# Two row blocks of an MLP's first layer by seven block products for eight, in a kernel that adds an FNet layer and an MLP

## The chip, the cores and the metric

The kernel runs on one core of a Trainium2 chip. The metric is the time of one execution in device microseconds (us). Engines are named as in the profile: PE is TensorE, DVE VectorE, ACT ScalarE, POOL GpSimd, SP the engine that issues most DMAs; ACT issues some.

## The reference

x has 2048 rows of 640. After a layer norm without scale or shift, two branches are added to x: the real part of a two-dimensional Fourier transform, given as matrices, and an MLP with 1536 hidden units.

```
xn = layernorm(x)
a, b = xn @ wr.T, xn @ wi.T                      # 640 x 640
y = cr @ a - ci @ b                              # 2048 x 2048
mlp = gelu(xn @ w1 + b1) @ w2 + b2               # tanh form of gelu
out = x + y + mlp
```

All is float32. A float32 product is made of three matmuls in the fp32r type: each operand is split into an upper half (a copy, rounded) and a lower half (the rest), and upper x upper, upper x lower and lower x upper are summed in PSUM (`product`, L269 to L274).

## The kernel before

The rows are worked on in four blocks of 512 (NT = 4, TB = 512), the hidden units in 12 groups of 128 (NF = 12), the 640 columns in 5 chunks of 128 (ND = 5). First the MLP runs for the four blocks, then the Fourier branch.

**MLP.** The main loop (L746 on) counts g from 0 to 47: block t and unit i. `hidden(g)` (L280) makes the first layer of one unit for one block in bank g % 3: 5 chunks x 3 matmuls of 128x512, one line, L292. `gelu(g)` (L301) has ACT apply gelu from PSUM into a buffer "ab", copy it to the upper half of "hs", and DVE subtract for the lower half. `output(g)` (L313) adds this unit's part of the second layer into banks 3 to 7: 5 x 3 matmuls. hidden runs two units ahead of output, so a unit goes hidden(g + 2), gelu(g + 2), output(g). Each engine executes its instructions in the order in which the program writes them; there is no scheduler.

The split weights W1 and W2 of all 12 units stay in SBUF from block 0 to the end of the MLP, in places (`PLACES`, L130) that the Fourier stages take over afterwards.

**Beside the MLP.** `background(t, i)` (L682) prepares the next block: rows of x are loaded (`load_x`), `ln_stats` takes their mean and variance on DVE, `ln_scale` one square root on ACT (which loads another table, and gelu's again), `ln_apply` normalises on DVE and stores each chunk of 128 rows to DRAM in four pieces, so 16 stores "xs" for a block, on SP. `load_z` reads them back in another order, and `transpose_z` and `prep_xt` turn and split them for the next block. For blocks 2 and 3 three of the four x chunks are loaded a block ahead, and 27 us or so lie between ln_apply and the first turn.

`prep_w(s)` (L381) has 15 steps in blocks 1 and 2 (`w_steps`, L743). They make seven forms of sums of the hidden transform's weights for each chunk j, for a seven-product scheme in the Fourier branch: step 3j turns two raw tiles on DVE and makes forms 0 and 1, step 3j + 1 forms 6 and 2, step 3j + 2 forms 3, 4 and 5. `put_w` (L366) makes one form: ACT copies the upper half into one of two buffers "wst", DVE subtracts, and ACT issues the store to DRAM ("wit"). Stores are issued in pairs at the end of a step's pair (`put_away`).

During block 3 `build` and `fourier_step` (L721) make the operands of the Fourier stages from the stored xs ("xab", "xc"), and store some to DRAM (forms_ab, forms_c).

At the end of a block `add_block` (L330) adds the bias on ACT in the bank, has DVE turn it into one of two buffers and POOL add it to the rows of x ("xo"), which go to DRAM ("ys").

Of the kernel before, what the change touches and what calls it, by code (L numbers as in the profile page):

```python
# [13 lines left out]
ALU = mybir.AluOpType  # L14
# [12 lines left out]
def kernel(  # L27
# [78 lines left out]
    def bank(k):  # L106
        return banks[:, k]
# [32 lines left out]
    ]  # L140
    slots = {}

    def place(tag, shape, dtype=F32R):

        return wpool.tile(list(shape), dtype, tag=tag, bufs=1, name=tag)
# [74 lines left out]

    def new_xt(t, j):
        XT[j] = mr.tile([P, 2, TB], F32R, tag="xt", bufs=ND, name=f"xt{t}_{j}")
# [8 lines left out]
    def transpose_z(t, j):  # L231
        zt[j] = mr.tile([P, TB], F32, tag="zt", bufs=2, name=f"zt{t}_{j}")
        nc.vector.transpose(
            zt[j].rearrange("p (n i) -> p n i", i=B), Z["z"][:, :, j * B : (j + 1) * B]
        )
# [41 lines left out]
    NG = NT * NF  # L277
    HT, oacc, xo = {}, {}, {}

    def hidden(g):  # L280
        i = g % NF
        acc = bank(g % 3)
        kinds = ((0, 0), (0, 1), (1, 0))
        steps = [(j, k) for j in range(ND) for k in range(3)]
        if g == 0:
            steps = FIRST
        if g == 1:

            steps.sort(key=lambda s: s[1] == 2)
        for n, (j, k) in enumerate(steps):  # L290
            a, b = kinds[k]
            nc.tensor.matmul(  # L292
                acc, W1[i][:, a, j * P : (j + 1) * P], XT[j][:, b], start=n == 0, stop=n == len(steps) - 1
            )
        return acc
# [5 lines left out]
    def gelu(g, acc, fill=lambda k: None):  # L301

        i = g % NF
        a = mr.tile([P, TB], F32, tag="ab", bufs=2, name=f"ab{g}")
        nc.scalar.activation(a, acc, AF.Gelu_apprx_tanh, bias=b1c[:, i : i + 1])  # L305
        fill(0)
        hs = mr.tile([P, 2, TB], F32R, tag="hs", bufs=3, name=f"hs{g}")
        HT[g] = hs
        nc.scalar.activation(hs[:, 0], a, AF.Copy)  # L309
        fill(1)  # L310
        nc.vector.tensor_tensor(hs[:, 1], a, hs[:, 0].bitcast(F32), op=ALU.subtract)  # L311

    def output(g):  # L313
        t, i = divmod(g, NF)
        if i == 0:
            oacc[t] = [bank(3 + e) for e in range(ND)]
        hs = HT[g]
        for e in range(ND):
            cols = slice(e * P, (e + 1) * P)
            product(  # L320
                oacc[t][e], (W2[i][:, 0, cols], W2[i][:, 1, cols]), (hs[:, 0], hs[:, 1]), i == 0, i == NF - 1
            )
# [7 lines left out]
    def add_block(dst, e, acc, name, eng=nc.gpsimd, bias=None, home=rows):  # L330

        if bias is not None:
            nc.scalar.activation(acc, acc, AF.Identity, bias=bias)
        yt = home.tile([P, TB], F32, tag="yt", bufs=2, name=name)
        nc.vector.transpose(yt, acc)
        d = dst[:, :, e * B : (e + 1) * B]
        eng.tensor_tensor(d, d, yt.rearrange("p (n i) -> p n i", i=B), op=ALU.add)
# [4 lines left out]
    def load_w(m, j):  # L342

        t = A["w"].tile([P, EB, B], F32, tag=f"wraw{m}", bufs=1, name=f"wraw{m}_{j}")
        A["wraw", m] = t
        v = (wr, wi)[m].rearrange("(n r) d -> r n d", r=B)
        for q in range(Q):
            s0 = q * DQ + j * B
            nc.sync.dma_start(t[q * B : (q + 1) * B], v[:, :, s0 : s0 + B])

    def turn_w(m, j):
        t = A["w"].tile([P, D], F32, tag=f"wt{m}", bufs=1, name=f"wt{m}_{j}")
        A["wt", m] = t
        nc.vector.transpose(
            t.rearrange("p (c q i) -> p q c i", q=Q, i=B),
            A.pop(("wraw", m)).rearrange("p (q c) i -> p q c i", q=Q),
        )

    stores = []
# [6 lines left out]
    def put_w(w, j, main, odd=None, negative=False):  # L366

        n = GWIDE[w] * P
        t = A["w"].tile([P, 2, 3 * P], F32R, tag="wst", bufs=2, name=f"wst{w}_{j}")
# [11 lines left out]
    def prep_w(s):  # L381
# [4 lines left out]
        if k == 0:  # L386
            turn_w(0, j)
            turn_w(1, j)
            if j + 1 < ND:
                load_w(0, j + 1)  # L390
                load_w(1, j + 1)
# [137 lines left out]
    def load_xr(k):  # L529
# [4 lines left out]
        if k in (0, len(builds) - 1):  # L534
            n = 2 if k else 0
            A["xcp", n] = place(f"xc{n}{n + 1}", (P, 2, 2, 7 * P))
# [9 lines left out]
    def build(k, what="abc"):  # L546
        h, c = builds[k]
        b0, b1_ = [r.rearrange("p (q c i) -> p c q i", q=Q, i=B) for r in xr[k]]
        if k == 0:
            A["sums"] = out_pool.tile([P, 2, 9 * P], F32, tag="zo", bufs=1, name="sums")  # L550
        if k < NK:
            A["xab", c] = place(f"xab{c}", (P, 2, 10 * P))
        A["xc", c] = A["xcp", c // 2 * 2 if h == 0 else 0][:, c % 2]
        ab, xc = A["xab", c], A["xc", c]
        tmp = A["sums"][:, k % 2]
# [40 lines left out]

    zeros = rows.tile([P, TB], F32, tag="yt", bufs=2, name="zeros")
# [25 lines left out]
    for tag, size, keys in PLACES:  # L623
        t = place(tag, (P, size // 4))
# [15 lines left out]
    scratch = mr.tile([P, 2 * TB], F32, tag="hs", bufs=3, name="scratch")[:, :D]  # L640
# [41 lines left out]
    def background(t, i):  # L682

        if t == 1 and i == 0:
            es_e.close()
            A["es"] = ExitStack()
            A["w"] = pool("wrawp", stack=A["es"])
            load_w(0, 0)
            load_w(1, 0)
        if t + 1 < NT:  # L690
            c0 = (t + 1) * NC

            s = 2 if t == 0 else 0
            if t == 0 and i < 2:
                ln_apply(2 * i)
                ln_apply(2 * i + 1)
                load_x(c0 + 2 * i)
                load_x(c0 + 2 * i + 1)
            elif t > 0 and i == 0:
                load_x(c0 + 3)  # L700
            if s <= i < s + 4:
                ln_stats(c0 + i - s)
            if i == s + 4:
                ln_scale(c0, 4)
                for c in range(c0, c0 + 4):
                    ln_apply(c)
                load_z(t + 1)
                if t + 2 < NT:
                    for c in range(c0 + 4, c0 + 7):
                        load_x(c)  # L710
            if i in (8, 9):
                transpose_z(t + 1, i - 8)
        if t == 3 and i == 0:
            A["es"].close()
            A["raw"] = pool("rawp")
            load_xr(0)
            load_xr(1)
            load_a(0)
            load_a(1)

    def fourier_step(i):  # L721
        if 2 <= i < 2 + 2 * NK:
            k = i - 2
            build(k, "abc" if i < 9 else "a")
            if k < NK:
                nc.sync.dma_start(forms_ab[k], A["xab", k].bitcast(F32))
                nc.sync.dma_start(forms_c[k], A["xc", k].bitcast(F32))
            load_xr(k + 2)
        if i == 9:
            A["r01"] = place("r01", (P, 2, 2, 2, TB), F32)  # L730
            turn(0, 0)
            turn(0, 1)
            A["as"] = place("as", (P, 3, 2, 2, TB))
        if i == 10:
            form(0)
            turn(1, 0)
            turn(1, 1)
            form(1)
        if i == 11:
            form(2)  # L740


    w_steps = [(1, i) for i in (1, 2, 3, 3, 5, 6, 7)] + [(2, i) for i in (0, 1, 2, 3, 5, 5, 6, 7)]  # L743
    gelu(0, acc0)
    gelu(1, acc1)
    for g in range(NG):  # L746
# [6 lines left out]
        background(t, i)  # L753
        if i == 10 and t + 1 < NT:
            load_xo(t)
        if i == NF - 1:
            acc = hidden(g + 2) if g + 2 < NG else None
            output(g)
            if acc is None:

                fourier_step(i)
                break

            def fill(k):
                for e in ((0,), (1, 2))[k]:
                    add_block(xo[t], e, oacc[t][e], f"ot{t}_{e}", bias=b2c[:, e : e + 1])

            gelu(g + 2, acc, fill)
            for e in (3, 4):
                add_block(xo[t], e, oacc[t][e], f"ot{t}_{e}", bias=b2c[:, e : e + 1])  # L770
            for k, (c0, c1) in enumerate(YCOLS):
                nc.sync.dma_start(ys[k][t], xo[t][:, :, c0:c1])
        elif i == NF - 2:
            output(g)
            if g + 2 < NG:
                gelu(g + 2, hidden(g + 2))
        else:
            acc = hidden(g + 2)
            if i == NF - 3 and t + 1 < NT:
                for j in range(ND):  # L780
                    prep_xt(t + 1, j)
                    if j + 2 < ND:
                        transpose_z(t + 1, j + 2)
            gelu(g + 2, acc)
            output(g)
        if t == 3 and i < NF - 1:
            fourier_step(i)
        for k, step in enumerate(w_steps):
            if step == (t, i):
                prep_w(k)  # L790
# [60 lines left out]
    for e in range(ND):  # L851
# [461 lines left out]
```

## Time and profile before

| | us |
|---|---|
| runs shown: median, lowest, highest | 860.79, 860.23, 860.89 |
| span of the profiled execution | 858.6 |
| median less that span: starting and ending | 2.2 |
| 15 matmuls (one unit, one layer) | 3.40 |
| blocks 1 to 3, from unit 0 to unit 0 | 81.6 |

The profile lists each engine's busy time, the chain of work that ended last, and groups of instructions with their mean duration (ns) and the idle time of their engine ahead of them, with what ended it. A matmul is shown with 389 ns, but they overlap in the array; one starts every 227 ns. In rows of the timeline the columns are start, length (us), engine, line, operation, output<-input, form, count, and in brackets the idle time ahead and what ended it. ACTq and SPq are the queues in which DMAs are issued. The profiled execution's own time is not listed beside its span; the three runs' median stands for it.

### The profile page before, as it was taken

How to read it: one execution, taken by the hardware profiler on the slowest of the kernel's cores; microseconds unless marked ns; L12 is line 12 of the kernel's file. 1: busy time of each engine (PE TensorE's matmuls, PEld its weight loads, DVE VectorE, ACT ScalarE, POOL GpSimd, SP SyncE). 2: the span in 40 equal slices, each digit the busy share in tenths (PEclk: the TensorE clock that was granted, in tenths of full speed). 3: DMA queues.
4: the chain of work that ended last, by engine and by line, in shares of the span. 5: the costliest groups of instructions: out<-in, count | busy, mean ns of one | idle time of the engine just before them, and what ended most of it. 6: DMA issues, size and time to landing. Idle time of an engine off the chain costs nothing.

```text
span 858.6 us, 10232 instructions
## 1 busy us (share of the span) xinstructions
PE 850.2 (99%) x3747; PEld 703.1 (82%) x3747; DVE 624.1 (73%) x792; ACT 335.7 (39%) x468; POOL 21.0 (2%) x22
## 2 busy tenths in 40 slices
PE   8999999999999999999999999999999999999997
PEld 6888888888888888888888888888888888888885
DVE  7554555366443678989989787998977998885687
ACT  7354434255333555443434344232322423223241
POOL 0000300030003000000000000000000000000000
PEclk9999999999999999999999999999999999999999
DMA  6656476875457984949753659954765879804364
GB/s 184 198 164 175 97 176 189 215 153 174 141 165 169 319 358 86 218 105 216 167 151 86 184 159 266 237 127 107 176 186 172 260 177 230 313 19 177 123 170 105
DMA packets 208625, 152.34 MB, mean 177 GB/s; under 512 B 82368, under 2 KB 182976, under 8 KB 208064
## 3 DMA queue, kind: packets, MB, share of 16 engines
q1 hardware_dynamic: 196336, 138.98, 62.4%
q10 hardware_dynamic: 12240, 12.72, 4.2%
q8 instruction: 29, 0.48, 0.2%
q14 instruction: 20, 0.16, 0.1%
HBM read 108.67 MB, written 42.99 MB: 177 GB/s over the span
## 4 chain that ended last, share of the span: by engine, by line
PE 98%; DMA 0%; DVE 0%; SPq 0%; issue 0%; ACT 0%; DVEq 0%; ACTq 0%
PE banks L273 26%; PE banks L272 26%; PE banks L274 26%; PE banks L292 19%; DMA x<-in_A_x_dram 0%; PE banks L635 0%; DVE st L185 0%; SPq L178 0%; DVE yo L1278 0%; DVE mv L186 0%; DVE xp L208 0%; ACT mv L192 0%; DVE mv L194 0%; DVE mv L195 0%; DVE mv L197 0%
## 5 line engine op out<-in xcount | busy, mean ns | idle before, releaser
L274 PE MATMUL banks<-as,xab 128*128 128x512 f32 x407 | 158.4, 389 | 0.0
L272 PE MATMUL banks<-as,xab 128*128 128x512 f32 x407 | 158.3, 389 | 0.0
L273 PE MATMUL banks<-as,xab 128*128 128x512 f32 x407 | 158.3, 389 | 0.0
L160 ACT ACTIVATE as<-r 128x1024 fp32r<-128x1024 f32 x80 | 85.0, 1062 | 173.1 <-PE banks L274 148.6
L161 DVE TENSOR_TENSOR as<-r,as 128x1024 fp32r<-128x1024 f32 x80 | 97.2, 1216 | 38.9 <-ACT as L160 38.9
L292 PE MATMUL banks<-xt,xab 128*128 128x512 f32 x420 | 99.1, 389 | 0.0
L311 DVE TENSOR_TENSOR hs<-ab,hs 128x512 fp32r<-128x512 f32 x48 | 36.5, 760 | 78.5 <-ACT hs L309 78.5
L292 PEld LDWEIGHTS banks<-xt,xab 128*128 128x128 f32 x420 | 78.7, 188 | 16.5 <-DVE xt L161 0.2
L272 PEld LDWEIGHTS banks<-as,xab 128*128 128x128 f32 x407 | 76.4, 188 | 16.0
L273 PEld LDWEIGHTS banks<-as,xab 128*128 128x128 f32 x407 | 76.4, 188 | 15.9
L274 PEld LDWEIGHTS banks<-as,xab 128*128 128x128 f32 x407 | 76.4, 188 | 15.8
L272 PE MATMUL banks<-as,xc 128*128 128x512 f32 x224 | 87.1, 389 | 0.0
L273 PE MATMUL banks<-as,xc 128*128 128x512 f32 x224 | 87.1, 389 | 0.0
L274 PE MATMUL banks<-as,xc 128*128 128x512 f32 x224 | 87.1, 389 | 0.0
L305 ACT ACTIVATE ab<-banks,b1c 128x512 f32<-128x512 f32 x48 | 33.0, 689 | 96.3 <-PE banks L292 91.8
L160 ACT ACTIVATE as<-rt 128x1024 fp32r<-128x1024 f32 x32 | 34.0, 1063 | 70.6 <-PE banks L274 57.9
L292 PE MATMUL banks<-xt,as 128*128 128x512 f32 x240 | 57.0, 389 | 0.0
L292 PEld LDWEIGHTS banks<-xt,as 128*128 128x128 f32 x240 | 45.0, 188 | 9.4
L272 PEld LDWEIGHTS banks<-as,xc 128*128 128x128 f32 x224 | 42.0, 188 | 8.8
L273 PEld LDWEIGHTS banks<-as,xc 128*128 128x128 f32 x224 | 42.0, 188 | 8.7
L274 PEld LDWEIGHTS banks<-as,xc 128*128 128x128 f32 x224 | 42.0, 188 | 8.7
L272 PE MATMUL banks<-hs,xc 128*128 128x512 f32 x120 | 46.7, 389 | 0.0
(170 smaller groups left out, 1365.5 us busy)
## 6 DMA issues: line engine op xcount, KB each, us to landing
raw<-in_A_dft_seq_re_dram SPq DMA_DIRECT2D x64, 256.0 KB, 5.9
raw<-in_A_dft_seq_im_dram SPq DMA_DIRECT2D x64, 256.0 KB, 5.4
wit<-wst ACTq DMA_DIRECT2D x20, 384.0 KB, 3.5
ws<-wit SPq DMA_DIRECT2D x15, 384.0 KB, 4.4
x<-in_A_x_dram SPq DMA_DIRECT2D x16, 320.0 KB, 4.3
xs<-x SPq DMA_DIRECT2D x64, 80.0 KB, 1.8
xo<-in_A_x_dram SPq DMA_DIRECT2D x16, 320.0 KB, 6.1
forms_ab<-xab SPq DMA_DIRECT2D x4, 1280.0 KB, 5.9
```

Source lines behind the costliest of these rows:

```text
L160: nc.scalar.activation(h, s, AF.Copy)
L161: nc.vector.tensor_tensor(l, s, h.bitcast(F32), op=ALU.subtract)
L272: nc.tensor.matmul(acc, wh, mh, start=first, stop=False, skip_group_check=goes_on)
L273: nc.tensor.matmul(acc, wh, ml, start=False, stop=False, skip_group_check=goes_on)
L274: nc.tensor.matmul(acc, wl, mh, start=False, stop=last, skip_group_check=goes_on)
L292: nc.tensor.matmul(acc, W1[i][:, a, j * P : (j + 1) * P], XT[j][:, b], start=n == 0, stop=n == len(steps) - 1)
L305: nc.scalar.activation(a, acc, AF.Gelu_apprx_tanh, bias=b1c[:, i : i + 1])
L311: nc.vector.tensor_tensor(hs[:, 1], a, hs[:, 0].bitcast(F32), op=ALU.subtract)
```

## The change

Blocks 0 and 1 stay as they are, but units 0 and 1 come last in block 1. For blocks 2 and 3 the first layer is made for both at once. Of the 5 chunks of x and the 12 units, the first four chunks (two halves, 1 and 2) and a pair of units (a, b) and the two row blocks make 2x2 by 2x2 blocks, and Winograd's form of Strassen's scheme makes their product in 7 block products for 8; the fifth chunk is multiplied plainly. For this the operands are sums: of x (a11, a12, a22, s1 to s4, made once, in block 1 and shortly behind it), and of w1 (t1 to t4, for each of six pairs q, from w1 loaded once more: `load_rq`, `sums_w1`, `split_w1`). A block product of the pair is 2 chunks x 3 matmuls; an odd one is 3.

A round q is `head`, `mid`, `finish`; the program writes mid(q), head(q + 1), finish(q). Five of the eight banks are a round's: y, d, x2, z2, w_. ACT copies y to x2 and to z2 while products are added to y (`copy_bank`), d to SBUF (`A["fifth"]`), which DVE adds to y and w_. So four units come out (two units, two blocks), whose gelu (`act`) is put into SBUF as float32 (`park`). prep_w's steps 0 to 5 run in block 1, 6 to 14 in rounds 1 to 4.

Then the second layers follow, block 2 and block 3, 12 units each: `split_h` makes both halves of two units at a time, W2 of units 2 to 10 is loaded and split again (`raw_w2`, `split_w2`), since its place held the operands of x; and `build` runs beside it (`beside_second`). Some tiles are now parts of one fixed tile (XTT, HS, AB, ZT).

The diff, cut to its core:

```diff
+    w_early = {1: (0,), 2: (1,), 3: (2,), 4: (3,), 5: (4, 5)}
...
+    def head(q):
+        y, d, x2, z2, w_ = PB[q]
+        pair(y, q, "b11", "a11", True)
+        copy_bank(x2, y)
+        pair(d, q, "t1", "s1", True)
+        nc.scalar.activation(A["fifth"], bank(d), AF.Copy)
...
+    def mid(q, between=lambda: None):
+        y, d, x2, z2, w_ = PB[q]
+        pair(y, q, "t2", "s2", False)
+        copy_bank(z2, y)
+        between()
+        pair(x2, q, "b21", "a12", False)
+        pair(x2, q, "o1", "oa", False)
+        if q % 2:
+            act(q, 0, 0)
+        pair(z2, q, "t3", "s3", False)
+        add(bank(y), bank(y), A["fifth"])
+        add(bank(w_), bank(z2), A["fifth"])
+
+    def finish(q):
+        y, d, x2, z2, w_ = PB[q]
+        pair(z2, q, "t4", "a22", False)
+        pair(z2, q, "o1", "ob", False)
+        pair(y, q, "b22", "s4", False)
+        pair(y, q, "o2", "oa", False)
+        pair(w_, q, "o2", "ob", False)
...
+    def second_block(i):
+        if i == 0:
+            open_w()
+            ln_scale(8, 4)
+            for c in range(8, 12):
+                ln_apply(c)
+            for c in range(12, 16):
+                load_x(c)
+        if i == 1:
+            load_z(2)
+        if 2 <= i < 6:
+            ln_stats(10 + i)
+        if i == 3:
+            A["zs"] = place("xc01", (P, 30 * P), F32, name="zs")
+            turn_z2(two(0), 0)
+            turn_z2(two(2), 2)
+        if i == 4:
+            turn_z1(ZT[:, 0], 4)
+            form_of("a11", 0, two(0)[:, 0], lane("as", 5))
+        if i == 6:
+            ln_scale(12, 4)
+            for c in range(12, 16):
+                ln_apply(c)
+            load_z(3)
...
+        if i == 7:
+            open_tw()
+            open_xf()
+        if i == 8:
+            turn_z2(ZT, 2)
+            turn_z2(two(4), 0)
+            turn_z1(A["zs"][:, 6 * TB : 7 * TB], 4)
+            sums_w1(0)
+        if i == 9:
+            load_xo(1)
+            split_w1(0)
+            load_rq(1)
+            form_of("a22", 0, ZT[:, 0], lane("r01", 0))
+            form_of("a22", 1, ZT[:, 1], lane("r01", 1))
+            add(ZT, ZT, two(4))
+            form_of("s1", 0, ZT[:, 0], lane("r01", 2))
+            form_of("s1", 1, ZT[:, 1], lane("r01", 3))
...
         elif i == NF - 2:
             output(g)
+            forms_s2()
+            head(0)
+            forms_s3()
         else:
             output(g)
...
+    sums_w1(1)
+    split_w1(1)
+    load_rq(2)
+    form_of("ob", 0, A["zs"][:, 6 * TB : 7 * TB], HS[:, 0])
+    outs(1, (0,), yt=lambda n: AB[:, 0], done=False)
+
+    def rest():
+        outs(1, (2, 1, 3, 4), yt=lambda n: AB[:, (n + 1) % 2])
+        add(two(2), two(2), ZT, ALU.subtract)
+
+    mid(0, rest)
+    forms_s4()
+    head(1)
+    finish(0)
+    open_wz()
+    late_steps = {1: (6, 7), 2: (8, 9), 3: (10, 11), 4: (12, 13, 14)}
+    for q in range(1, NF // 2):
+        p = q - 1
+        if not p % 2:
+            act(p, 0, 0)
+        sums_w1(q + 1)
+        act(p, 0, 1)
+
+        def between():
+            split_w1(q + 1)
+            act(p, 1, 0)
+            act(p, 1, 1)
+
+        mid(q, between)
+        for k in late_steps.get(q, ()):
+            prep_w(k)
+        load_rq(q + 2)
+        if q < NF // 2 - 1:
+            head(q + 1)
+        else:
+            split_h(0)
+            second(2, 0, 0, HU[0, 0])
+            split_h(1)
...
+        finish(q)
...
+    def beside_second(n):
+
+        if n % 2 and 2 <= (n + 3) // 2 < NF:
+            split_h((n + 3) // 2)
+        if 1 <= n <= 6:
+            late_w2(n + 4)
+        if n in (2, 4, 6, 8):
+            formed(n // 2 - 1)
+            load_xr((2, 3, 4, 6)[n // 2 - 1])
...
+        if n == 11:
+            outs(2, (3, 4, 0, 1, 2))
...
+    for n in range(1, 2 * NF):
+        blk, i = divmod(n, NF)
+        if blk == 0:
+            second(2, i, i, HU[0, i])
+        elif i == 0:
+            for es in ((0, 1, 2), (3, 4)):
+                for k in range(2):
+                    second(3, k, LATE[k], HU[1, LATE[k]], es)
+        elif i > 1:
+            second(3, i, LATE[i], HU[1, LATE[i]])
+        beside_second(n)
```

More of the change, by code (lines that the diff above doesn't have):

```diff
@@ L274, in product, with unit @@
         nc.tensor.matmul(acc, wl, mh, start=False, stop=last, skip_group_check=goes_on)
-    NG = NT * NF
+    NG = 2 * NF
+    LATE = [*range(2, NF), 0, 1]
     HT, oacc, xo = {}, {}, {}
+    def unit(g):
+        return g if g < NF else LATE[g % NF]
     def hidden(g):
-        i = g % NF
+        i = unit(g)
         acc = bank(g % 3)
@@ L679 @@
     load_w1(5)
[L682 to L719, printed above, removed]
@@ new lines, in pair, with copy_bank @@
+    def pair(k, q, w, x_, first):
+        n = 1 if x_ in ("oa", "ob") else 2
+        for cc in range(n):
+            f = FX[x_, cc]
+            product(bank(k), weights(q, w, cc), (f[:, 0], f[:, 1]), first and cc == 0, cc == n - 1, not first)
+    PB = [[0, 1, 2, 3, 4]]
+    for _ in range(5):
+        y, d, x2, z2, w_ = PB[-1]
+        o = [k for k in range(8) if k not in PB[-1]] if len(PB) == 1 else left
+        PB.append([o[0], o[1], o[2], d, x2])
+        left = [y, z2, w_]
+    def copy_bank(dst, src):
+        nc.scalar.activation(bank(dst), bank(src), AF.Copy)
@@ L752 @@
             load_w2(i + 4)
[L753 to L757, printed above, removed]
-            output(g)
[L759 to L772, printed above, removed]
+            first_block(i)
@@ new lines, with fill @@
+            if i == 10:
+                load_xo(0)
+            if i == NF - 1:
+                acc = hidden(g + 2)
+                output(g)
+                def fill(k):
+                    for e in ((0,), (1, 2))[k]:
+                        add_block(xo[0], e, oacc[0][e], f"ot0_{e}", bias=b2c[:, e : e + 1])
+                gelu(g + 2, acc, fill)
+                outs(0, (3, 4))
+            elif i == NF - 2:
+                output(g)
+                gelu(g + 2, hidden(g + 2))
+            else:
+                acc = hidden(g + 2)
+                if i == NF - 3:
+                    for j in range(ND):
+                        prep_xt(1, j)
+                        if j + 2 < ND:
+                            transpose_z(1, j + 2)
+                gelu(g + 2, acc)
+                output(g)
+        elif i < NF - 2:
+            acc = hidden(g + 2)
+            gelu(g + 2, acc)
+            output(g)
+            second_block(i)
+            for k in w_early.get(i, ()):
+                prep_w(k)
@@ new lines, with formed @@
+    act(5, 0, 1)
+    act(5, 1, 0)
+    act(5, 1, 1)
+    A["esx"].close()
+    es_rows = ExitStack()
+    rows = pool("rows2", side="right", stack=es_rows)
+    load_xr(0)
+    load_xr(1)
+    A["asb"] = place("as", (P, 48 * P), name="asb")
+    A["sums"] = A["asb"][:, 20 * P : 38 * P].bitcast(F32).rearrange("p (a b) -> p a b", a=2)
+    def formed(k):
+        build(k)
+        nc.sync.dma_start(forms_ab[k], A["xab", k].bitcast(F32))
+        nc.sync.dma_start(forms_c[k], A["xc", k].bitcast(F32))
```

330 lines of the change are left out of this document (267 added, 63 removed), and 10 rows, old and new, of the table PLACES.

## The prediction

> **What bounds the kernel now.** The page first:
>
> ```profile
> span 858.6 us, 10232 instructions
> PE 850.2 (99%) x3747; PEld 703.1 (82%) x3747; DVE 624.1 (73%) x792; ACT 335.7 (39%) x468; POOL 21.0 (2%) x22
> PE 98%; DMA 0%; DVE 0%; SPq 0%; issue 0%; ACT 0%; DVEq 0%; ACTq 0%
> ```
>
> TensorE is busy for 99% of the span and is 98% of the chain that ended last: time goes only if matmuls go, and any wait that TensorE gets is added in full. The chain in order of time gives the rhythm:
>
> ```profile
> 100.89 3.40 PE banks L292 x15
> 107.69 3.40 PE banks L292 x15
> ...
> 162.09 3.40 PE banks L292 x15
> ```
>
> Fifteen matmuls take 3.40 us, 0.2267 each. Block 1's unit i starts at 100.89 + 6.80 i: 3.40 for hidden, 3.40 for output, no gap. ScalarE is busy 39% of the time, but what counts for it below is how long its queue stands. For that I read its timeline where two steps of prep_w follow each other, in two places, and the first six steps from end to end:
>
> ```profile
> 115.20 0.62 ACT L160 ACTIVATE wst<-wt 128x256 fp32r<-128x256 f32 x2 [2.72 <-DVE wt L354]
> ...
> 127.50 0.42 ACT L160 ACTIVATE wst<-wt 128x256 fp32r<-128x256 f32 x1 [0.81 <-DMA wit<-wst]
> ...
> 135.40 0.36 ACTq L377 DMA_DIRECT2D wit<-wst  x1
> ...
> 150.89 0.52 ACTq L377 DMA_DIRECT2D wit<-wst  x1
> ...
> 221.22 0.71 ACT L160 ACTIVATE wst<-wt 128x256 fp32r<-128x256 f32 x2
> 222.40 1.20 ACTq L377 DMA_DIRECT2D wit<-wst  x2
> 226.17 0.42 ACT L160 ACTIVATE wst<-wt 128x256 fp32r<-128x256 f32 x1 [4.24 <-DMA wit<-wst]
> 227.07 0.52 ACTq L377 DMA_DIRECT2D wit<-wst  x1
> 227.96 0.62 ACT L160 ACTIVATE wst<-wt 128x256 fp32r<-128x256 f32 x2 [1.37 <-DVE wt L354]
> ...
> 230.69 0.33 ACTq L377 DMA_DIRECT2D wit<-wst  x1
> ...
> 245.85 0.52 ACTq L377 DMA_DIRECT2D wit<-wst  x1
> ```
>
> Two steps hold the queue from 127.50 to 135.76 (8.3 us) and from 221.22 to 231.02 (9.8 us), though the instructions in them run for about half of that. There are two wst buffers: a third form waits until the first store has landed, and a store waits for VectorE's subtraction. Three steps, 227.96 to 246.37, hold it 18.4 us, in which two gelu pairs of 1.3 us each stand: 15.8 without them. Today no matmul waits for this: a gelu that is late has the two units after it as cover, some 10 us.
>
> **The change, part by part.** Durations that I use, from the groups of instructions by line and shape:
>
> ```profile
> L161 DVE TENSOR_TENSOR as<-r,as 128x1024 fp32r<-128x1024 f32 x80 | 97.2, 1216 | 38.9 <-ACT as L160 38.9
> ...
> L474 DVE STREAM_TRANSPOSE r<-raw 128x1024 f32<-128x1024 f32 x32 | 39.5, 1239 | 0.6
> ...
> L305 ACT ACTIVATE ab<-banks,b1c 128x512 f32<-128x512 f32 x48 | 33.0, 689 | 96.3 <-PE banks L292 91.8 <-DVE wt L414 2.6 <-DVE wst L161 1.9
> ...
> L337 POOL TENSOR_TENSOR xo<-xo,ot 128x512 f32<-128x512 f32 x15 | 20.2, 1382 | 248.2 <-DVE ot L335 172.7 <-DMA xo<-in_A_x_dram 75.5
> ...
> L160 ACT ACTIVATE as<-rt 128x1024 fp32r<-128x1024 f32 x32 | 34.0, 1063 | 70.6 <-PE banks L274 57.9 <-issue 6.3 <-DVE rt L414 4.7
> ...
> L335 DVE STREAM_TRANSPOSE ot<-banks 128x512 f32<-128x512 f32 x15 | 10.7, 715 | 12.6 <-ACT banks L333 9.7 <-POOL xo L337 2.9
> ...
> L333 ACT ACTIVATE banks<-banks,b2c 128x512 f32<-128x512 f32 x15 | 9.2, 664 | 0.0
> ...
> L161 DVE TENSOR_TENSOR xc<-w2r,xc 128x640 fp32r<-128x640 f32 x6 | 4.9, 817 | 0.0
> ```
>
> *Removed.* A pair of units for two blocks took 4 x 15 = 60 matmuls; now seven products of six and four odd ones of three are 54. Six pairs save 36 (the built program has 3711 for 3747): 36 x 0.2267 = **-8.2 us**. Nothing hides this; it is all that can be gained. A round of 54 lasts 12.24 us.
>
> *Rounds.* In each round ScalarE does three bank copies (not in the trace; nearest L333, 0.66), four gelus (0.69) and the upper half of the W1 sums (1.06): 5.8 us. Two steps of prep_w stand in the same queue, behind the gelus and **ahead of** the copy of bank y that head(q + 1) has filled. TensorE goes on with finish(q), 21 matmuls, and then its first matmul of mid(q + 1) writes y, and waits for that copy. So a round lasts as long as ScalarE's queue: 5.8 + 9.8 = 15.6 us against 12.24, 3.4 late. Rounds 1, 2 and 3 have two steps each: 10.2. Round 4 has three: 5.8 + 15.8 = 21.6, 9.4 late. Together **+19.6**. Queued behind the copy are the fifth bank's copy and the next gelus, so nothing is made good later. With the 8.3 us stretch (and 13.3 for three) the sum is 1.9 x 3 + 6.9 = 12.6; if each of some twelve waits for a store were as long as the 4.24 one, about 2 us more than I have, it is over 30. I take the 9.8 row, since loads of w stand beside these steps as they did there.
>
> *Block 1.* Its DMAs move up the SP queue:
>
> ```profile
> 62.46 7.37 SPq L203 DMA_DIRECT2D xs<-x  x16
> ...
> 112.11 2.16 SPq L349 DMA_DIRECT2D wraw<-in_A_dft_hid_im_dram  x4
> ...
> 141.31 13.36 SPq L203 DMA_DIRECT2D xs<-x  x16
> ...
> 213.90 16.97 SPq L203 DMA_DIRECT2D xs<-x  x16
> ```
>
> ```profile
> 79.72 0.71 DVE L233 STREAM_TRANSPOSE zt<-z 128x512 f32<-128x512 f32 x1 [5.82 <-DMA z<-xs]
> ...
> 121.23 0.69 DVE L311 TENSOR_TENSOR hs<-ab,hs 128x512 fp32r<-128x512 f32 x1 [0.55 <-ACT hs L309]
> ...
> 167.49 0.71 DVE L233 STREAM_TRANSPOSE zt<-z 128x512 f32<-128x512 f32 x1 [10.69 <-DMA z<-xs]
> ```
>
> ```profile
> x<-in_A_x_dram SPq DMA_DIRECT2D x16, 320.0 KB, 4.3
> ```
>
> From the first store of xs to z in SBUF: 62.46 to 79.72 is 17.3 us, 141.31 to 167.49 is 26.2. Now rows 12 to 15 of x are asked for in unit 0, behind eight loads of w (issued until 114.27) and 16 stores (7.4 to 17.0; I take 10): 124.3, and 4.3 to land, 129. VectorE comes to their statistics at 121.9 and stands 7 us, with prep_w(1) behind it. The six steps that ended at 151.41 get these 7, two turns of z2 (2.5), and the a11 form, transposes and waits that these push: about 163. gelu(20) and its halves take 2 more, 165; output(20) wants them at 155.29 + 3.40 = 158.7: TensorE stands 6. Then square root, scale and ln_apply, some 3: 168; the shorter chain through xs, 17.3: z3 at 185. Behind that wait on VectorE: turns 3.2, W1 sums 1.4, the last lower half 0.7, the W1 split 2.3, two forms 1.3, an add 1.2, the s1 form: about 10, so s1 at 195. head(0)'s second pair wants it at 162.09 + 3 x 3.40 + 1.36 = 173.65, or 180 with the 6 lost already. Sum **+21**. If nothing is late ahead of the scale, z3 comes at 149.5 + 17.3 and s1 at 176.8: 3. With 26.2 for the chain: 30. I keep 21, by the chain as worked out.
>
> *Between.* Behind s1 VectorE has twelve more us (sums and lower halves for s2 and s3, the second W1 pair) before it turns block 1's first output bank, which the third product overwrites; TensorE has 8.2 us of matmuls until there: 4 to 5 late with the copy. Then four more banks go out at POOL's 1.38, with two buffers, ahead of the two adds of the fifth bank that finish(0) waits for: 2 to 3 more. **+7**; 2 to 9.
>
> *Second layers.* split_h(0) has no cover (1.7). Until bank 3 is free for block 3, VectorE has six splits (1.2), six W2 lower halves (0.8), four builds and two shorter ones in eleven units of 3.40:
>
> ```profile
> 283.15 0.42 DVE L414 TENSOR_TENSOR sums<-xr 128x256 f32<-128x256 f32 x1
> ...
> 287.19 0.83 DVE L414 TENSOR_TENSOR xc<-sums,xc 128x640 fp32r<-128x640 f32 x1 [0.47 <-ACT xc L566]
> ```
>
> a build is 4.9, so 7.3 + 4.9 + 19.5 + 6 = 37.7 in 37.4, then two transposes: about 2.3 late. **+4**; 0 with slack, 9 if the stores of the forms hold the one xcst buffer.
>
> Block 0, the Fourier stages and the tail keep their work: 0, as their covers are those of before.
>
> **Sum:** 858.6 - 8.2 + 19.6 + 21 + 7 + 4 = 902.0. The median of the runs, 860.79, is 2.2 over the profiled span, with starting and ending around it: **904 us**.
>
> **The rivals.** *Only the rounds stall* (27 in 100): x 12 to 15 land in time and block 1 keeps its floor of 3. For it: xs took 7.37 once. 858.6 - 8.2 + 19.6 + 3 + 4 + 2 + 2.2 = 881.
>
> *A cold clock on top* (15): the first matmuls of the run are slow:
>
> ```profile
> 1.91 7.03 PE L616 MATMUL banks<-warm 128*128 128x512 f32 x19 [1.91 <-DVE warm L607]
> ```
>
> 0.370 each for 0.2267. If each of some seven long waits cost as much again, 7.03 - 19 x 0.2267 = 2.7, it is 19 more: 923. The granted clock on the page never shows it (full speed throughout), and the waits may be too short. [...]
>
> *Faster* (9): the stores land early enough that two steps fit into what a round leaves, 12.24 - 5.8 = 6.4 us, and z3 comes in time. The deciding point is 6.4 against the 8.3 and 9.8 seen; a pair's own instructions are about 4.7, so nothing but landing times forbids it. 858.6 - 8.2 + 3 + 2.2 = 856. Waits that happen to add up to 8 (no change): 3. Slower by less than 10 us: 6. That fewer matmuls go than claimed is excluded by the count.
>
> **How the numbers follow.** 904 has 40 in 100. The range takes in 881 and its lower rounds sum (12.6 for 19.6: 874) and above the cold clock with part of the longer z chain: 872 to 930; left out are the 9, 3 and 6 and a little above. A measurement of this kernel can tell about 0.2%, 1.7 us. Faster 0.09, same 0.03, slower 0.88.
>
> **What would show it.** 3711 matmuls; gaps on TensorE before the first matmul of rounds 2 to 5, released by ScalarE's copy, some 3 us and the last near 9; ScalarE waiting in prep_w for stores in those rounds; VectorE waiting for rows of x in unit 2 and about 10 us for z3; one gap of over 10 us ahead of the first t1 product. If TensorE shows no gap at the copies, the step on the queue is wrong; if the six steps end near 151, the one on block 1.

## The result, and the profile after

The changed kernel takes **940.06 us** (median of 4 runs, 938.47 to 941.35), the kernel before 860.56 in the same session: a ratio of 1.0923, with a 95% interval of 1.0908 to 1.0939. The forecast was 904 and its range ended at 930: the direction was right, the size was not.

From the page of the changed kernel, the span, the busy times, the clock granted in 40 slices of 23.5 us, and the chain that ended last:

```profile
span 938.7 us, 10279 instructions
...
PE 866.1 (92%) x3711; PEld 707.4 (75%) x3711; DVE 660.8 (70%) x831; ACT 354.4 (38%) x495; POOL 22.0 (2%) x22
...
PEclk9999999978987899989999999999999999999999
...
PE 58%; DMA 8%; DVE 4%; ACT 2%; SPq 2%; issue 1%; POOL 1%; POOLq 0%; ACTq 0%; DVEq 0%
```

The span is 80.1 us longer. TensorE does 36 matmuls less, as forecast, which is 8.2 us. It stands 938.7 - 866.1 = 72.6 us for 8.4 before, so 64.2 more. And the 3711 matmuls, which would take 850.2 - 8.2 = 842.0 by the rate of before, are busy for 866.1: **24.1 us more**. -8.2 + 64.2 + 24.1 = 80.1. The forecast had 51.6 us of waits and nothing for slower matmuls. The clock row tells why they are slower: it is at 7 or 8 in six slices, where that of the kernel before has 9 in all forty:

```profile
PEclk9999999999999999999999999999999999999999
```

What TensorE waited for, by the line that released it (us in all, times, longest):

```profile
PE banks L277 <- ACT banks L801: 24.0, 5, 10.4
PE banks L277 <- ACT r L160: 14.6, 1, 14.6
PE banks L277 <- ACT hs L318: 6.5, 2, 4.1
PE banks L277 <- ACT xtt L160: 5.5, 1, 5.5
PE banks L277 <- DVE ot L347: 5.2, 1, 5.2
PE banks L277 <- ACT pb L845: 4.4, 2, 3.2
```

In the order of the rows: the copies of bank y (L801), one of them in round 0 (3.9), the other four ahead of rounds 2 to 5 (20.1 together); the s1 form ahead of the first t1 product; the halves of hs for output(18) and output(20); two late waits in the second layers (a split of gelu values, and the drain of bank 3); and two gelus of the rounds. Now the clock, in windows of 20 us (length, TensorE busy and its matmuls, granted clock, share of the DMA engines, GB/s), and the first matmuls after the wait ahead of round 5 (start, duration):

```profile
160.00:180.00 20.00, 15.66 (x62) 0.91 0.43 124
180.00:200.00 20.00, 5.41 (x22) 0.71 0.84 170
200.00:220.00 20.00, 16.07 (x53) 0.77 0.26 64
...
300.00:320.00 20.00, 13.25 (x43) 0.71 0.33 103
```

```profile
305.34 0.79 PE L277 MATMUL banks<-xfx,tw 128*128 128x512 f32 x1 [10.43 <-ACT banks L801]
305.93 0.63 PE L278 MATMUL banks<-xfx,tw 128*128 128x512 f32 x1
306.36 0.63 PE L279 MATMUL banks<-xfx,tw 128*128 128x512 f32 x1
```

After eight of the waits the matmuls follow each other at 0.425 us, for 0.2267 in the kernel before; 72 of them do so in the whole trace. The granted clock is at half for 61 us of the 938.7, in eight stretches in mid-run; 37.5 us of them lie behind the end of a wait, where TensorE works, and half of that, 18.7, is lost. The rest of the 24.1, 5.4 us, no run separates.

### The profile page after: what moved, and what is told of

The parts are those of the page before. It is cut to its first block, busy times and chain, and to the rows that moved or that the text cites. A ratio compares the mean times of both kernels' runs of the same rounds, so it can differ in the third digit from the quotient of the medians.

```text
span 938.7 us, 10279 instructions
## 1 busy us (share of the span) xinstructions
PE 866.1 (92%) x3711; PEld 707.4 (75%) x3711; DVE 660.8 (70%) x831; ACT 354.4 (38%) x495; POOL 22.0 (2%) x22
## 4 chain that ended last, share of the span: by engine, by line
PE 58%; DMA 8%; DVE 4%; ACT 2%; SPq 2%; issue 1%; POOL 1%; POOLq 0%; ACTq 0%; DVEq 0%
PE banks L278 19%; PE banks L277 19%; PE banks L279 19%; DMA wit<-hs 3%; DMA forms_c<-xcst 2%; DMA xo<-in_A_x_dram 1%; DMA xr<-xs 1%; SPq L477 1%; DVE hs L161 1%; POOL xo L349 1%; DMA rq<-in_B_w_dram 1%; DVE asb L437 0%; DVE rq L437 0%; ACT xcst L589 0%; DVE rt L497 0%
## 5 line engine op out<-in xcount | busy, mean ns | idle before, releaser
L278 PE MATMUL banks<-as,xab 128*128 128x512 f32 x411 | 160.2, 390 | 0.8 <-DVE as L161 0.8
L279 PE MATMUL banks<-as,xab 128*128 128x512 f32 x411 | 160.2, 390 | 0.0
L277 PE MATMUL banks<-as,xab 128*128 128x512 f32 x411 | 160.1, 390 | 0.0
L278 PEld LDWEIGHTS banks<-as,xab 128*128 128x128 f32 x411 | 77.3, 188 | 17.4 <-DVE as L161 1.2
L279 PEld LDWEIGHTS banks<-as,xab 128*128 128x128 f32 x411 | 77.3, 188 | 16.1
L277 PEld LDWEIGHTS banks<-as,xab 128*128 128x128 f32 x411 | 77.3, 188 | 16.0
L301 PE MATMUL banks<-xtt,xab 128*128 128x512 f32 x240 | 56.7, 390 | 0.0
L301 PEld LDWEIGHTS banks<-xtt,xab 128*128 128x128 f32 x240 | 44.9, 188 | 9.5 <-DVE xtt L161 0.2
L320 DVE TENSOR_TENSOR hs<-ab,hs 128x512 fp32r<-128x512 f32 x24 | 17.6, 735 | 40.2 <-ACT hs L318 40.1
L161 DVE TENSOR_TENSOR as<-rt,as 128x1024 fp32r<-128x1024 f32 x32 | 38.8, 1212 | 5.3 <-ACT as L160 5.3
L497 DVE STREAM_TRANSPOSE r<-raw 128x1024 f32<-128x1024 f32 x32 | 39.5, 1240 | 1.5 <-PE banks L279 1.0
L160 ACT ACTIVATE as<-u 128x1024 fp32r<-128x1024 f32 (+1 forms) x24 | 22.1, 919 | 48.2 <-PE banks L279 48.2
L437 DVE TENSOR_TENSOR r<-r,rt 128x1024 f32<-128x1024 f32 x32 | 38.9, 1219 | 0.1
```

The lines of the kernel that those rows point to most:

```text
L160: nc.scalar.activation(h, s, AF.Copy)
L161: nc.vector.tensor_tensor(l, s, h.bitcast(F32), op=ALU.subtract)
L277: nc.tensor.matmul(acc, wh, mh, start=first, stop=False, skip_group_check=goes_on)
L278: nc.tensor.matmul(acc, wh, ml, start=False, stop=False, skip_group_check=goes_on)
L279: nc.tensor.matmul(acc, wl, mh, start=False, stop=last, skip_group_check=goes_on)
L301: nc.tensor.matmul(acc, W1[i][:, a, j * P : (j + 1) * P], XT[j][:, b], start=n == 0, stop=n == len(steps) - 1)
```

## The experiments

**Theory.** Steps of prep_w that stood beside 6.80 us units now stand in rounds of 12.24 us with three copies in the same queue, and ahead of z3. They hold ScalarE by the landing of their stores, and hold what stands behind them on SyncE and VectorE; the longer waits that this makes on TensorE are followed by a stretch at half clock. **Rivals.** The matmuls of the changed kernel are slow for a reason of their own; the transfers of x, xs and raw w1 set the times, whatever the steps do.

**The later steps left out.** In rounds 1 to 4, in place of `prep_w(k)`:

```
-        for k in late_steps.get(q, ()):
-            prep_w(k)
+        for s in late_steps.get(q, ()):
+            for w in ((0, 1), (6, 2), (3, 4, 5))[s % 3]:
+                nc.sync.dma_start(wits[w][s // 3], HS[:, 1, :, : GWIDE[w] * P].bitcast(F32))
```

> The changed kernel with the nine later steps of prep_w left out of rounds 1 to 4 (their w forms are not computed; something else of the same size is stored by SyncE in their place). Queue theory: the copies of bank y are then in time; the 20.1 us of waits for copies in rounds 2 to 5 and the 4.4 us of waits for gelus go, and with them the half-clock stretches that follow them, some 8 us: 940 falls to about 908. Rival (the copies are late for another reason, by the W1 sums on VectorE or the transfers of raw w1): the gaps ahead of rounds 2 to 5 stay and the time is over 930.

904.95 us (1.0520, 1.0497 to 1.0542): 35.1 less. The first matmul of the t2 products in rounds 1 to 3 of this run:

```profile
228.49 0.39 PE L277 MATMUL banks<-xfx,tw 128*128 128x512 f32 x1
...
240.73 0.39 PE L277 MATMUL banks<-xfx,tw 128*128 128x512 f32 x1
...
252.97 0.39 PE L277 MATMUL banks<-xfx,tw 128*128 128x512 f32 x1
```

A round is 12.24 us, with no wait. In the changed kernel the same instructions start at 225.43, 240.56, 258.51, 280.80 and 305.34: rounds of 15.1, 18.0, 22.3 and 24.5. The queue theory holds, and the steps cost more than the waits for copies: 20.1 for those, 4.4 for the gelus, and some 10 of slower matmuls (TensorE is busy for 856.0 us where it was 866.1). The steps' own loads of w went with them, so this run does not tell ScalarE's queue from SyncE's; two runs below do.

**The early steps left out.** The same replacement in units 1 to 5 of block 1.

> The changed kernel with the six early steps of prep_w left out of units 1 to 5 of block 1 (their w forms are not computed; something else of the same size is stored by SyncE). Theory (the steps on VectorE and ScalarE make z3 and the s1 form late): output(18) and output(20) no longer wait (2.4 and 4.1 us), the wait of 14.6 us ahead of the first t1 product falls to some 3, and with them some 7 us of half clock go: about 915. Rival (rows 12 to 15 of x and the trip through xs hold z3 whatever VectorE does): the long wait stays over 10, and the time is over 928.

917.93 us (1.0659, 1.0635 to 1.0682): 22.1 less. Of TensorE's waits in block 1 one row is left:

```profile
PE banks L277 <- ACT r L160: 3.4, 1, 3.4
```

That is the floor of 3 that the prediction gave for z3 when nothing is late ahead of the scale. The trips of x and xs alone do not hold it for longer.

**Spare matmuls in place of the waits.** Six waits, those of rounds 2 to 5 and two of round 0 (60 and 15 matmuls), are filled with matmuls into a bank that is overwritten next:

```
+    SPARE = {2: 10, 3: 13, 4: 14, 5: 44}
...
+        if q in SPARE:
+            spare(z2, q, SPARE[q])
         pair(y, q, "t2", "s2", False)
```

> The changed kernel with spare matmuls, whose result is overwritten, in place of the idle time at six waits: 60 ahead of the t1 products of round 0, 15 ahead of its t3 products, and 10, 13, 14 and 44 ahead of the t2 products of rounds 2 to 5. They take no more time than TensorE has waited there. Clock theory: the waits keep their ends, but no half-clock stretch follows them; those places have about 44 of the 61 us at half clock, so some 17 us (13 to 20) go: 940 falls to about 923. Rival (matmuls are slower there for another reason, their operands or the traffic of the DMAs): 940 or more, since the spare matmuls add work and the slow ones stay slow.

933.90 us (1.0849, 1.0833 to 1.0865): 6.2 less, though TensorE does 156 matmuls more. The matmuls that follow the filled waits start every 0.23 us, and those at 0.425 fall from 72 to 40: the rival falls. But only 6 of the forecast 17 came back. I had shared the 24 us out by the length of the half-clock stretches, and counted 44 us at the filled places where there are 37.5. Of these only 18.8 lie behind the end of a wait, so that 9.4 were to be had; the rest, 10.5 us in the 14.6 us wait alone, lies inside the waits, where it costs nothing. One wait that was not filled even gained a stretch: it is 1.62 us long, and at 250.73 the clock falls to half for 3.41 us.

```profile
249.49 0.50 PE L277 MATMUL banks<-r,tw 128*128 128x512 f32 x1 [1.62 <-ACT pb L856]
```

**The kernel before, with waits put in.** Eight units of blocks 2 and 3 get a wait ahead of their second layer's matmuls, and nothing else:

```
+    HOLD = {25: 1, 27: 2, 29: 3, 31: 4, 37: 2, 39: 3, 41: 6, 43: 16}
...
             gelu(g + 2, acc)
+            for _ in range(HOLD.get(g, 0)):
+                h = HT[g][:, 0]
+                nc.scalar.activation(h, h.bitcast(F32), AF.Copy)
             output(g)
```

> The kernel before, with eight waits put into blocks 2 and 3 where TensorE had none: at units 25, 27, 29, 31, 37, 39, 41 and 43 ScalarE rewrites the upper half of hs in place 1, 2, 3, 4, 2, 3, 6 and 16 times ahead of the second layer's matmuls. By 1.35 + 0.66 us a time, with 0.3 for the passing of semaphores, the waits are about 2.3, 3.0, 3.6, 4.3, 3.0, 3.6, 5.6 and 12.2 us, 37.6 in all. Clock theory: waits of some 3 us and under leave the clock alone, each of the longer ones brings at least one stretch of 3.4 us at half clock (two or more for the longest), which costs 1.6 us each where TensorE works in it: 37.6 + about 9, 907 in all. Rival (only the changed kernel's own work slows its matmuls): 860.8 + 37.6 = 898, with the granted clock at full speed throughout.

910.25 us (1.0575, 1.0557 to 1.0593), 49.4 more than before, for 36.1 us of waits: 13.3 us, or **37% on top**. The waits are 1.30 us and 0.66 for each rewriting, but for the fourth, which is longer; the 0.3 us that I had expected for the passing of semaphores does not show. The first waits, and the clock in windows behind each:

```profile
194.56 0.50 PE L272 MATMUL banks<-hs,xc 128*128 128x512 f32 x1 [1.96 <-ACT hs L788]
...
211.07 0.80 PE L272 MATMUL banks<-hs,xab 128*128 128x512 f32 x1 [2.62 <-ACT hs L788]
...
229.58 0.50 PE L272 MATMUL banks<-hs,xc 128*128 128x512 f32 x1 [3.28 <-ACT hs L788]
...
250.39 0.80 PE L272 MATMUL banks<-hs,r 128*128 128x512 f32 x1 [5.25 <-ACT hs L788]
```

```profile
194.50:201.00 6.50, 6.45 (x28) 1.00 0.34 120
211.00:214.50 3.50, 3.43 (x9) 0.58 0.62 180
229.50:236.00 6.50, 6.42 (x21) 0.74 0.45 147
250.30:257.00 6.70, 6.61 (x20) 0.66 0.34 118
```

28 matmuls fit behind the wait of 1.96 us; in windows about as long, 21 and 20 fit behind 3.28 and 5.25. Over all eight waits 25.9 us at half clock lie behind the end of a wait, and half of that, 13.0, is the 13.3. Nothing but the waits was put in, so this kernel's own matmuls do it as well. The length of a wait does not settle it: behind 1.96 us the clock is full, while 2.62 was enough twice here, and 1.62 once in the run before.

**Two chains in a round.** First, one line moved, then five buffers for the later forms in place of two:

```
+        load_rq(q + 2)
         for k in late_steps.get(q, ()):
             prep_w(k)
-        load_rq(q + 2)
```

```
-            t = HS[:, 1 + A["nst"] % 2, :, : 3 * P]
+            t = A["five"][:, A["nst"] % 5]
...
+        A["five"] = place("xc01", (P, 5, 2, 3 * P), name="five")
```

> The changed kernel with one line moved: in a round, the load of raw w1 for two rounds on (load_rq) is issued ahead of the steps of prep_w and not behind them. Theory (two chains hold a round: the stores in ScalarE's queue, and raw w1, which stands on SyncE behind the loads of w that wait for the steps' transposes; the split of its sums waited 3.7 and 5.7 us, with the gelus behind it): the waits of the split go, the rounds get about 9 us shorter in all, 931 or a little under. Rival (ScalarE's queue alone sets a round): within 4 us of 940.

> The changed kernel with five buffers for the w forms of the later steps, in the 15 KB of xc01 that nothing uses in rounds 1 to 4, in place of the two in hs. Theory (a step is long because its third form waits for the first one's store: 25.3 us of such waits in nine steps): ScalarE's share of a round falls to some 11 us, under the 12.24 of TensorE, and most of the 35 us that leaving the steps out has saved is saved here: about 914. Rival (VectorE's part of the steps and raw w1 behind the loads of w hold the round just as long): over 928.

932.57 (1.0837, 1.0806 to 1.0868) and 924.31 us (1.0748, 1.0728 to 1.0768): 7.5 and 15.8 less. Both chains are real; the five buffers alone bring less than forecast (924 for 914), since the other chain holds then. ScalarE's waits for the sums of raw w1 in the rounds (us, times, longest), with raw w1 first and with five buffers:

```profile
ACT tw L160 <- DVE rq L437: 2.4, 1, 2.4
```

```profile
ACT tw L160 <- DVE rq L437: 14.8, 3, 6.9
```

The first is in ScalarE's timeline of the changed kernel, round 4 (waits in brackets): forms wait until an earlier one's store has landed, and the copy that TensorE wants stands behind them all:

```profile
290.17 1.19 ACTq L400 DMA_DIRECT2D wit<-hs  x2
294.75 0.42 ACT L160 ACTIVATE hs<-wz 128x256 fp32r<-128x256 f32 x1 [4.46 <-DMA wit<-hs]
...
298.95 0.42 ACT L160 ACTIVATE hs<-wz 128x256 fp32r<-128x256 f32 x1 [2.15 <-DMA wit<-hs]
...
303.23 0.42 ACT L160 ACTIVATE hs<-wz 128x256 fp32r<-128x256 f32 x1 [2.75 <-DMA wit<-hs]
...
304.70 0.58 ACT L801 ACTIVATE banks<-banks 128x512 f32<-128x512 f32 x1 [1.05 <-DVE hs L161]
```

The second is in SyncE's timeline and the chain in order of time, round 2: the loads of w (L364) wait for the steps' transposes, raw w1 (L747) stands behind them, and the split of its sums and the gelus behind that:

```profile
254.58 2.06 SPq L364 DMA_DIRECT2D wz<-in_A_dft_hid_re_dram  x4
256.74 2.84 SPq L364 DMA_DIRECT2D wz<-in_A_dft_hid_im_dram  x4
259.82 10.71 SPq L747 DMA_DIRECT2D rq<-in_B_w_dram  x8
```

```profile
262.10 2.58 DMA rq<-in_B_w_dram
...
264.80 0.70 DVE rq L437
...
266.45 1.06 ACT tw L160
```

**The second layers.** In a first run only loads were moved (xo for block 2 to n = 7, raw pieces behind xr5); in a second also build 6 and a staging buffer:

```
-        if n == 10:
-            build(6, "ab")
...
             outs(2, (3, 4, 0, 1, 2))
+            build(6, "ab")
...
+    homes_c[3] = lambda: A["tw"].tile([P, 2, 7 * P], F32R, tag="tw0", bufs=1, name="xcst3")
```

> The changed kernel with two moves in the second layers: xo for block 2 is loaded one unit earlier (n = 7, ahead of the stores and loads of n = 8), and the first two raw pieces are loaded behind xr5 (n = 14) instead of ahead of it (n = 11). Theory (both late waits of TensorE there, 5.2 and 5.5 us, come from the order of SyncE's queue): both go, and the half-clock stretches behind them, some 5 us: about 924. Rival (bank 3 is late because of VectorE's backlog or the stores of the forms): only the second wait goes, and the time is about 931.

> The changed kernel with the two moves of loads in the second layers (xo at n = 7, raw pieces behind xr5 at n = 14), the ab part of build 6 moved behind the drains of block 2's banks (n = 11 for 10), and the forms of build 3 staged in a buffer of their own. Theory (bank 3's drains stood on VectorE behind the split that stood behind build 6, whose xr waited for the fourth use of one staging buffer): both waits (5.2 and 5.5 us) go and their half-clock stretches with them: about 924. Rival (the staging buffer's first three uses hold split_h and the W2 splits as well, so that the drains stay late): 930 or more.

935.49 (1.0864, 1.0846 to 1.0883) and 922.63 us (1.0726, 1.0704 to 1.0747). With loads alone the second wait went, and bank 3's grew from 5.2 to 8.7: there my first theory fell, with 4.6 us saved for 16. With all of it both went, 17.4 us for 10.7 us of waits. The chain of the changed kernel shows the one staging buffer, store by store, and xo's load behind the last:

```profile
333.10 5.77 DMA forms_c<-xcst
...
340.90 5.63 DMA forms_c<-xcst
...
348.57 5.76 DMA forms_c<-xcst
...
361.78 8.83 DMA xo<-in_A_x_dram
```

Bank 3 does not wait for xo: its drain ends at 370.0, and xo lands at 370.6. It waits for the rows of build 6, which SyncE asks for behind the stores, and for which VectorE stands 4.9 us ahead of the drain. xo's load belongs to the chain of the second wait.

```profile
364.74 0.42 DVE L437 TENSOR_TENSOR asb<-xr 128x256 f32<-128x256 f32 x1 [4.89 <-DMA xr<-xs]
```

**Block 1's order.** The scale, ln_apply and load of z3 from unit 6 to unit 5, ahead of steps 4 and 5; then also the statistics of rows 12 to 15 from units 2 to 5 into units 4 and 5.

```
-        if 2 <= i < 6:
-            ln_stats(10 + i)
+        if i in (4, 5):
+            ln_stats(4 + 2 * i)
+            ln_stats(5 + 2 * i)
```

> The changed kernel with the scale, the ln_apply of rows 12 to 15 and the load of z3 moved from unit 6 to unit 5 of block 1, ahead of steps 4 and 5 of prep_w. Queue theory: z3 comes some 10 us earlier, the wait of 14.6 us ahead of the first t1 product falls to about 5, and a half-clock stretch or two with it: about 928. Rival (the trips of x and of xs through DRAM set z3, not VectorE's queue): the wait stays and the time is 937 or more.

> The changed kernel with two moves in block 1: the statistics of rows 12 to 15 are done in units 4 and 5 (two each) and not one each in units 2 to 5, and scale, ln_apply and the load of z3 follow at once in unit 5, ahead of steps 4 and 5. Theory (VectorE stood 6.7 us for rows of x with prep_w's step behind it): the early steps end some 7 us earlier than in the run that only put z3 first, output(20) waits 3 for 10, and the time is about 923. Rival (the steps wait for their stores whatever comes before, or x lands later still): the same 931 as that run.

931.62 (1.0822, 1.0805 to 1.0839) and 931.83 us (1.0833, 1.0815 to 1.0851): 8.4 less and no more. The wait of 14.6 us goes, and output(20) waits 10.2, then 12.1, for 4.1: a step that is not ahead of z3 is ahead of a gelu. In the second run VectorE stood 12.7 us for z2 instead of 6.7 for x, and the forecast 923 did not come.

**All moves together,** and then four more in block 1 and the rounds:

```
+                load_w(0, j + 1, nc.scalar if j == 0 else nc.sync)
...
+    w_early = {1: (0,), 2: (1,), 3: (2,), 4: (3,), 5: (4,), 6: (5,)}
...
             head(q + 1)
+            if q == 4:
+                prep_w(14)
```

> The changed kernel with all the moves of the earlier runs together (raw w1 ahead of the steps, five buffers for the later forms, the second layers' order and staging buffer, the order of block 1), and the turns of z2 moved from unit 3 to unit 4, since VectorE stood 12.7 us for z2 in unit 3 of the last run. The whole computation is done. Theory (three separate stages, each with its own waits): the savings add up, 33 in the rounds (leaving the steps out saved 35), 17.4 in the second layers, 8 to 12 in block 1: 878 to 882. Rival (a wait that goes in one stage comes back in the next, since the same queues carry it on): over 890. Under 860 is not expected from either: block 1 and the passage to the rounds still hold some 20 us.

> The whole computation, with the moves of the last but one run (all moves) and four more: the second pair of raw w loads is issued by ScalarE and not behind the rows of x and z2 on SyncE; the early steps stand one in each of units 1 to 6; rows 12 to 15 are scaled in unit 5 ahead of the turns of z2 and the fifth step; step 14 stands behind head(5), and the drain of block 1's first bank ahead of the W1 sums. Theory (what is left are the wait of 11.8 us ahead of output(20), 5.5 ahead of round 5, 4.9 in round 0, and 10 us of half clock behind them): the first two go and a part of the third, with 8 of the 10: 863 (858 to 872). Rival (VectorE has more to do in block 1 than its units hold, whatever the order): one wait of about 10 us stays somewhere ahead of round 0, and the time is over 875.

889.49 (1.0331, 1.0314 to 1.0348) and 889.05 us (1.0330, 1.0316 to 1.0344). Most of the savings add up (50.6 of some 60, so 889 and not the 878 to 882 of the forecast), the second layers fill, the rounds too but for one wait of 5.5 us ahead of round 5, and block 1 stays. The second set did nothing: my 863 was wrong and its rival's number, over 875, came. What TensorE waited for in the two, in order:

```profile
PE banks L277 <- ACT hs L318: 11.8, 1, 11.8
PE banks L277 <- ACT banks L802: 10.7, 3, 5.5
```

```profile
PE banks L277 <- ACT hs L318: 8.8, 2, 6.4
PE banks L277 <- ACT banks L802: 8.2, 4, 4.4
PE banks L277 <- ACT r L160: 1.4, 1, 1.4
```

In the last run the chain in order of time goes through stores of the early forms (start, time to landing):

```profile
128.98 7.78 DMA wit<-wst
...
170.14 6.16 DMA wit<-wst
```

So the rival's number came, but not the one wait of about 10 us that it named (the longest is 6.4), and its reason may be the landings and not VectorE's load. More buffers for the early forms were not tried, and this stays open.

**No steps at all,** with the second layers in order:

> The changed kernel with all fifteen steps of prep_w left out (no w forms are computed; SyncE stores something else of the same size), raw w1 ahead of them in the rounds and the order and staging buffer of the second layers. The removed 8.2 us, the early steps (22.1 measured alone), the later ones (35.1) and the second layers (17.4) would make 940.1 - 74.6 = 865.5 if they add up. Theory: they do, and what is left over 860.8 - 8.2 = 852.6 is the passage from block 1 to the rounds, 3 to 4 us ahead of s1 and 4 to 6 in round 0, with a stretch or two of half clock: 862 to 867. Rival (with the steps gone the rounds and the second layers fill up without a wait, and the passage was late only because of what came before): 856 or less. Second rival (the stages were covering for each other): over 872.

868.87 us (1.0102, 1.0084 to 1.0120), 3.4 above the sum and 1.9 above the range of the first theory. What TensorE still waits for:

```profile
PE banks L277 <- ACT banks L807: 3.5, 1, 3.5
PE banks L277 <- ACT r L160: 3.5, 1, 3.5
...
PE banks L277 <- DVE banks L442: 1.4, 1, 1.4
PE banks L278 <- DVE hs L161: 1.1, 1, 1.1
```

The passage from block 1 to round 0 is a cost of its own, and with 5.7 us of slower matmuls (847.7 busy for 842.0) it alone takes more than the 8.2 that the fewer matmuls bring. Even with the steps for nothing the changed kernel would be no faster than the one before, but some 1% slower.

## Why the prediction was wrong, step by step

| step | forecast | measured |
|---|---|---|
| removed | -8.2 | -8.2: 3711 matmuls |
| rounds | +19.6 | waits for copies 20.1, for gelus 4.4; all that goes with the steps 35.1 |
| block 1 | +21 | waits 2.4 + 4.1 + 14.6 = 21.1; 22.1 without the steps, and 3.4 left |
| between | +7 | 3.9 for the copy; 3.5 + 1.4 without the steps |
| second layers | +4 | waits 1.4 + 5.2 + 5.5; 17.4 for the two late ones |
| slower matmuls | 0 in the sum | +24.1 |

**The step that failed** is the one that put *a cold clock on top* at 15 in 100 and at nothing in the sum. It measured 24.1 us, two thirds of the 36 that were missing. I argued that "the granted clock on the page never shows it". That page was of a kernel whose TensorE waited only at the start (1.9 and 1.0 us) and never in mid-run, so it could not show it. The slow first matmuls, 0.370 each for 0.2267, were at hand and pointed the right way. When waits were put in, the kernel before showed 13.3 us for eight. In the changed kernel it was more, 24.1 for eight waits with such a stretch, and the rival's 19, an estimate from those first matmuls, was nearer. With it in the sum the forecast would have been 923; what is missing to 940 is the rest of the 24.1, and the 12.6 us of waits below.

**Second layers** were mis-sized: +4 for 12.1 us of waits. I counted VectorE's instructions against the units and found 2.3 late. What held it were landings: four builds one after the other through one staging buffer at 5.6 to 5.8 us a store, with the rows of build 6 behind them, and on SyncE xo's load behind the last of them and xr5 behind raw pieces. I had that buffer as an upper bound of 9 and left out what stands behind it.

**Rounds**: the mechanism and the waits for copies were right to half a microsecond in the sum, partly by luck (2.7, 3.4, 3.6 and 10.4 for 3.4, 3.4, 3.4 and 9.4). The first round was as long as I gave (15.1 for 15.6), the later ones were longer (18.0 and 22.3 for 15.6, 24.5 for 21.6). The second chain, raw w1 behind the loads of w on SyncE, was not in my list of queues, and a late split delays gelus as well, which TensorE then waits for (4.4).

**Block 1** was right in detail: VectorE waited 6.7 for rows of x (7 forecast) and 14.2 for z3 (about 10), the six steps ended at 165 (163), z3 was turned at 189.0 (185), the first t1 product came at 199.0 (195). **Between** was right within its range. Waits in all: 64.2 for 51.6, so 12.6 more, which with 24.1 makes the 36 us between 904 and 940.

## What to carry to other kernels

The waits put ahead of a TensorE that was never idle in mid-run cost more than their length, here 37% more, so price the slow stretch behind a wait even where the profile of before shows a full clock. The steps that store through two small buffers were held by the landing of their stores (25.3 us of ScalarE's waits in the rounds), and moving them into a shorter loop moved their loads in SyncE's queue too (raw w1 behind the loads of w): list what stands behind each. Where fewer matmuls are bought by moving work that had cover, add up the covers first: 8.2 us were to be gained, and the early steps, the later ones and the second layers cost some 75 (22.1, 35.1 and 17.4, each measured alone).

## What the runs showed of the hardware

In the changed kernel the granted clock is at half for 61 us, in eight stretches of 3.41, 6.83, 10.24 or 13.65 us. They do not begin with the waits: four begin at 168.08, 188.56, 212.45 and 267.07, which is 20.48, 23.89 and 54.62 us apart (6, 7 and 16 times 3.41), and the waits there end at 167.09, 199.04, 213.08 and 268.13. A single length of the wait does not decide: in the kernel before with waits, the clock in the windows above is 1.00 behind 1.96 us, 0.58 behind 2.62 and 0.66 behind 5.25; in the changed kernel 2.73 and 3.36 brought no stretch and 3.19 did; with spare matmuls 1.62 brought one, without the early steps 1.93. In TensorE's timelines of the changed kernel and of ten of the runs, matmuls at 0.425 us follow no wait under 1.62 us, each of the 47 from 3.38 us on, and 16 of the 29 in between. With 156 matmuls into a bank that is overwritten next in place of six waits, the matmuls behind each of the six started every 0.23 us, and the run took 6.2 us less and not more. A store of a w form landed in 2.3 us at best, and took 6.2 to 7.8 in the rows above, from block 1 with the steps spread.
